# Shifting one ring of weight buffers by 64 bytes in the on-chip memory

## The chip, the cores and the metric

The kernel runs on one core of a Trainium2 chip. A core has a matrix engine (TensorE, PE in the profile; its weight loads are listed apart as PEld), a vector engine (VectorE, DVE), an activation engine (ScalarE, ACT), a general engine (GpSimd, POOL) and a queue engine that issues transfers (SyncE, SP). They work from an on-chip memory of 128 partitions (SBUF); TensorE writes its results to a second one (PSUM). The metric is the device time of one execution in microseconds, as the median of several runs; lower is better.

## The reference

A retention layer (attention without softmax, with a decay mask) feeds two feed-forward layers one after the other:

```python
def _attn_ref(q, k, v):                       # (4, 8, 576, 64) each
    scores = scale * np.matmul(q, k.transpose(0, 1, 3, 2))
    Dmat = np.where(rel >= 0, gamma[:, None, None] ** rel[None, :, :], 0.0)
    return np.matmul(scores * Dmat[None, :, :, :], v)

def _moe_ref(x, w_in, w_out):                 # x (2304, 512), w_in (512, 2048), w_out (2048, 512)
    h = x @ w_in
    return np.maximum(0.01 * h, h) @ w_out

def _moe2_ref(x, w_in, w_out):
    h = x @ w_in
    return (h - np.tanh(h)) @ w_out
```

The weights come as 64-bit floats; everything else is 32-bit.

## The kernel before

**Precision.** Each product of the two feed-forward layers is made of three matmuls in the one-pass form of 32-bit floats: a number is split into a high part (rounded to that form) and the rest, and high by high, high by rest and rest by high are added up in PSUM. So a split weight piece is a tile `wp` of 128 partitions x 2 x 512 floats: `wp[:, 0, :]` is the high part, `wp[:, 1, :]` the rest. Input activations stand split too, in `xh` and `xl`; the hidden layer's in `g`.

**Stages.** `retention()` handles 16 pairs of heads. For each it loads `qk` and `kv`, scales them on GpSimd, makes scores, masks them, and writes the result into `xh` and `xl`. From the fifth pair on it also runs pieces of the first feed-forward layer in blocks of 256 tokens (`unit_h`, L520, and `unit_o`, L545), as soon as the tokens are there. `layers()` then walks a list of steps: a step is one block of 512 or 256 tokens by one of the 16 slices of 128 hidden units; four slices make a group. `h_mm` (L195) makes 12 matmuls with a slice of `wp` as the stationary operand and `xh` or `xl` as the moving one. In the first layer `o_mm` (L267) has `wp` stationary and `g` moving; in the second the roles are exchanged, `g` stationary and the whole 512 columns of a `wp` half moving.

**The ring of split weights.** `split_piece` (L172 to L179) fills a tile of the pool `wring`: ScalarE writes the high part (L175), GpSimd reads the raw piece and the high part and writes the rest (L176). The pool has four buffers of each of two tags (`w0` for the incoming weights, `w1` for the outgoing ones), 4,096 bytes per partition each, 32,768 bytes in all. 64 pieces pass through it. Raw pieces (64-bit) are loaded into `st` (two buffers, L110) and turned into 32-bit floats in `cw` by VectorE; some are parked in memory (`kept`, L164) and fetched again (L169).

**Where buffers stand.** Pools are laid one behind the other in the order in which they are opened: `keep` (`qb`, `xh`, `xl`, `acc`, for the whole program), `wring`, `stage` (`st`), and then the pools of the stage that runs. All sizes in `keep` and behind it are multiples of 128 bytes per partition (`LINE` is 32 floats; small tables are rounded up to it), so every tile begins on a multiple of 128 bytes. The ring begins at byte 127,232 of each partition, which is 994 x 128. Slices of a tile that TensorE reads begin at further multiples of 256 bytes.

**Order.** Every engine works off its instructions in the order in which the code issues them; no scheduler changes it.

Of the kernel before, what the change touches and what calls it, by code (L numbers as in the profile page):

```python
# [10 lines left out]
F32 = mybir.dt.float32  # L11
# [7 lines left out]
P = 128  # L19
LINE = 32  # L20
# [14 lines left out]
def retention_moe_moe(  # L35
# [28 lines left out]
    keep = ctx.enter_context(tc.tile_pool(name="keep", bufs=1))  # L64
    wring = ctx.enter_context(tc.tile_pool(name="wring", bufs=GF))
    stage = ctx.enter_context(tc.tile_pool(name="stage", bufs=2))
# [2 lines left out]
    xh = keep.tile([P, KK, NT], F32R, name="xh")  # L69
    xl = keep.tile([P, KK, NT], F32R, name="xl")  # L70
    acc = keep.tile([P, KK * NT], F32, name="acc")
    acc_t = acc.rearrange("p (d t) -> p d t", d=KK)
    acc_n = acc.rearrange("p (t e) -> p t e", e=DM)

# [692 lines left out]
```

## Time and profile before

| | before |
|---|---|
| median of 3 runs | 894.48 us (893.25 to 894.73) |
| profiled execution, whole | 892.59 us |
| its span, first to last instruction | 890.8 us |
| TensorE matmul busy | 865.0 us, 97% |
| TensorE weight load busy | 741.6 us, 83% |
| VectorE / ScalarE / GpSimd busy | 60% / 42% / 47% |
| mean granted TensorE clock | 0.996 of full speed |

The span is the time between the first and the last instruction; 1.8 us of the execution lie outside it. The busy share of TensorE says little by itself, since matmuls overlap their neighbours' ends; the step from one matmul's start to the next is read from the chain of waits, which gives a stretch of equal matmuls as one piece with its length and count.

### The profile page before, as it was taken

What the parts mean: (1) busy time and instruction counts of PE and PEld (TensorE: products, weight loads), DVE (VectorE), ACT (ScalarE), POOL (GpSimd) and SP (SyncE); (2) the same over time, 40 slices, a digit from 0 to 9 for tenths busy, and PEclk for the clock granted to TensorE, in tenths of its full rate; (3) what the DMA queues carried; (4) which work ended last, traced back from release to release, by engine and by line L of the source; (5) the groups of instructions that cost most, each with busy time, mean ns of one, the idle gap of its engine ahead of it and who ended that gap; (6) DMA issues with size and microseconds to landing.
All of it is one profiled execution on the core that took longest, in us unless ns stands there. A gap on an engine that the chain in (4) does not pass through costs nothing.

```text
span 890.8 us, 13456 instructions
## 1 busy us (share of the span) xinstructions
PE 865.0 (97%) x5152; PEld 741.6 (83%) x5152; DVE 534.9 (60%) x880; ACT 374.5 (42%) x751; POOL 423.0 (47%) x340
## 2 busy tenths in 40 slices
PE   6669999999999999999999999999999999999998
PEld 6659999988888889888888888888888888888886
DVE  6964334698888788875652555444545655555454
ACT  2333222243122212233324656675466555565553
POOL 4544432264223622363224644585457744585443
PEclk9989999999999999999999999999999999999999
DMA  8633332223465345631121200020001000001111
GB/s 301 239 130 124 107 120 90 71 96 118 130 179 152 109 134 148 178 107 48 47 83 36 60 1 1 3 78 15 1 1 47 13 1 1 1 1 48 48 48 71
DMA packets 28575, 70.97 MB, mean 80 GB/s; under 512 B 3296, under 2 KB 3680, under 8 KB 28512
## 3 DMA queue, kind: packets, MB, share of 16 engines
q1 hardware_dynamic: 27936, 69.74, 24.3%
q8 instruction: 40, 0.66, 0.3%
q10 hardware_dynamic: 576, 0.38, 0.1%
q14 instruction: 23, 0.19, 0.1%
HBM read 59.10 MB, written 11.01 MB: 79 GB/s over the span
## 4 chain that ended last, share of the span: by engine, by line
PE 92%; DVE 3%; ACT 1%; DMA 1%; POOL 1%; issue 1%; SPq 0%; POOLq 0%; ACTq 0%
PE h L195 40%; PE a L267 40%; PE a L545 4%; PE x_b L520 3%; PE sc L406 1%; PE o L467 1%; PE o L479 1%; DVE cw L149 1%; DVE pt L421 1%; DMA kv<-in_vn 1%; POOL wp L176 1%; PE x_c L439 1%; DMA qk<-in_qT 0%; PE x_a L412 0%; DVE st L449 0%
## 5 line engine op out<-in xcount | busy, mean ns | idle before, releaser
L195 PE MATMUL h<-xh,wp 128*128 128x512 f32 (+1 forms) x1184 | 355.2, 366 | 0.0
L195 PEld LDWEIGHTS h<-xh,wp 128*128 128x128 f32 x1184 | 216.1, 189 | 36.8
L195 PE MATMUL h<-xl,wp 128*128 128x512 f32 (+1 forms) x592 | 216.9, 366 | 0.0
L267 PE MATMUL a<-wp,g 128*128 128x512 f32 x864 | 209.4, 390 | 0.2 <-POOL g L241 0.2
L267 PEld LDWEIGHTS a<-wp,g 128*128 128x128 f32 x864 | 161.1, 188 | 33.8 <-POOL g L241 1.0
L267 PE MATMUL a<-g,wp 128*128 128x512 f32 (+1 forms) x816 | 175.6, 364 | 0.0
L241 POOL TENSOR_TENSOR g<-v,g 128x512 fp32r<-128x512 f32 (+1 forms) x80 | 95.0, 1187 | 144.7 <-ACT g L240 144.6
L267 PEld LDWEIGHTS a<-g,wp 128*128 128x128 f32 x816 | 141.4, 189 | 24.6
L241 POOL TENSOR_TENSOR g<-a,g 128x512 fp32r<-128x512 f32 (+1 forms) x68 | 88.3, 1298 | 154.7 <-ACT g L209 141.3
L208 ACT ACTIVATE a<-h 128x512 f32<-128x512 f32 (+1 forms) x68 | 37.3, 549 | 227.0 <-PE h L195 226.0
L176 POOL TENSOR_TENSOR wp<-cw,wp 128x512 fp32r<-128x512 f32 x64 | 91.2, 1434 | 76.5 <-ACT wp L175 76.3
L195 PEld LDWEIGHTS h<-xl,wp 128*128 128x128 f32 x592 | 111.6, 189 | 18.6
L149 DVE SCALAR_TENSOR_TENSOR cw<-st,cw 128x512 uint32<-128x512 uint32 x128 | 116.9, 913 | 3.8
L234 DVE TENSOR_TENSOR h<-h,t 128x512 f32<-128x512 f32 (+1 forms) x80 | 51.5, 644 | 107.2 <-ACT t L218 107.2
L293 DVE TENSOR_TENSOR acc<-a,acc 128x512 f32<-128x512 f32 (+1 forms) x114 | 73.8, 663 | 65.2 <-PE a L267 65.2
L240 ACT ACTIVATE g<-v 128x512 fp32r<-128x512 f32 (+1 forms) x80 | 47.1, 589 | 145.4 <-DVE v L238 144.2
L219 POOL TENSOR_TENSOR v<-t,u 128x512 f32<-128x512 f32 (+1 forms) x80 | 94.8, 1185 | 14.0 <-ACT t L218 13.6
L235 DVE SCALAR_TENSOR_TENSOR v<-q,v 128x512 f32<-128x512 f32 (+1 forms) x80 | 55.6, 695 | 55.2 <-POOL v L219 54.2
L238 DVE COPY_PREDICATED v<-mk,h 128x512 f32<-128x512 uint32 (+1 forms) x80 | 55.0, 687 | 8.2
L220 ACT ACTIVATE q<-u,qb 128x512 f32<-128x512 f32 (+1 forms) x80 | 54.5, 681 | 0.0
L223 ACT ACTIVATE mk<-u,qb 128x512 f32<-128x512 f32 (+1 forms) x80 | 54.2, 678 | 0.0
L132 DVE TENSOR_SCALAR cw<-st 128x512 uint32<-128x512 uint32 x56 | 39.0, 696 | 22.0 <-DMA st<-in_w2i 8.5
(60 smaller groups left out, 781.1 us busy)
## 6 DMA issues: line engine op xcount, KB each, us to landing
st<-in_w1i SPq DMA_DIRECT2D x16, 512.0 KB, 3.7
st<-in_w1o SPq DMA_DIRECT2D x16, 512.0 KB, 3.4
st<-in_w2i SPq DMA_DIRECT2D x16, 512.0 KB, 3.9
st<-in_w2o SPq DMA_DIRECT2D x16, 512.0 KB, 3.9
kept<-cw SPq DMA_DIRECT2D x24, 256.0 KB, 4.2
cw<-kept SPq DMA_DIRECT2D x24, 256.0 KB, 2.6
kv<-in_vn SPq DMA_DIRECT2D x16, 320.0 KB, 4.9
qk<-in_qT SPq DMA_DIRECT2D x16, 288.0 KB, 3.7
```

The lines of the kernel that those rows point to most:

```text
L149: nc.vector.scalar_tensor_tensor(out=t["w"], in0=t[src], scalar=scalar, in1=t["w"], op0=op, op1=ALU.bitwise_or)
L176: nc.gpsimd.tensor_tensor(out=wp[:, 1, :], in0=wf, in1=wp[:, 0, :].bitcast(F32), op=ALU.subtract)
L195: nc.tensor.matmul(out=ps[:, :n], lhsT=w[:, wi, cs], rhs=x[:, kk, t0:t0 + n], start=kk == 0 and i == 0, stop=kk == KK - 1 and i == 2,)
L219: nc.gpsimd.tensor_tensor(out=v[:, :n], in0=t_[:, :n], in1=u[:, :n], op=ALU.mult)
L220: nc.scalar.activation(out=q[:, :n], in_=u[:, :n], func=AF.Square, scale=math.sqrt(RHO_C), bias=qb[:, 0:1])
L223: nc.scalar.activation(out=mk[:, :n], in_=u[:, :n], func=AF.Relu, bias=qb[:, 1:2])
L234: nc.vector.tensor_tensor(out=h, in0=h, in1=t_, op=ALU.subtract)
L235: nc.vector.scalar_tensor_tensor(out=v, in0=q, scalar=RHO_A, in1=v, op0=ALU.add, op1=ALU.mult)
L238: nc.vector.copy_predicated(out=v, mask=mk.bitcast(U32), data=h)
L241: nc.gpsimd.tensor_tensor(out=gt[:, 1, :n], in0=v, in1=gt[:, 0, :n].bitcast(F32), op=ALU.subtract)
L267: nc.tensor.matmul(out=o, lhsT=l, rhs=r, start=f == 0 and i == 0 and d % pack == 0, stop=f == GF - 1 and i == 2 and (d + 1) % pack == 0, s ...
L293: nc.vector.tensor_tensor(out=dst, in0=a, in1=dst, op=ALU.add)
```

## The change

Two small tiles that nothing writes or reads are added, 64 bytes per partition each:

```diff
@@ -69,6 +69,8 @@
     xh = keep.tile([P, KK, NT], F32R, name="xh")
     xl = keep.tile([P, KK, NT], F32R, name="xl")
     acc = keep.tile([P, KK * NT], F32, name="acc")
+    keep.tile([P, LINE // 2], F32, name="shift")
+    stage.tile([P, LINE // 2], F32, name="unshift", bufs=1)
     acc_t = acc.rearrange("p (d t) -> p d t", d=KK)
     acc_n = acc.rearrange("p (t e) -> p t e", e=DM)
```

The first stands at the end of `keep`, so the ring behind it begins at byte 127,296, 64 bytes behind a multiple of 128. The second stands at the beginning of `stage`, so `st` and all that follows moves by 128 bytes in all and begins on multiples of 128 as before. `qb`, `xh`, `xl` and `acc` stay where they were. One thing else shifts with it: what begins on a multiple of 256 bytes behind the ring (`st`, `g` and `cw` of the layers) begins on an odd multiple of 128 afterwards, and the other way round (`qk` and `kv` of the retention stage). No instruction is added, removed or moved on any engine; line numbers behind the two lines grow by 2.

## Rows read from the trace of the kernel before

**Rows 1.** The page's busy times, and the clock in 40 slices.

```profile
PE 865.0 (97%) x5152; PEld 741.6 (83%) x5152; DVE 534.9 (60%) x880; ACT 374.5 (42%) x751; POOL 423.0 (47%) x340
PEclk9989999999999999999999999999999999999999
```

**Rows 2.** Busy time by stretch: us, engines with counts, granted clock, DMA share, GB/s.

```profile
0.00:163.00 163.00, 141.31 (x1694) 132.02 (x1695) 84.14 (x212) 48.09 (x125) 67.84 (x56) 0.98 0.45 152
163.00:891.00 728.00, 723.68 (x3460) 609.60 (x3459) 450.79 (x668) 326.42 (x626) 355.13 (x284) 1.00 0.20 63
...
40.00:90.00 50.00, 41.14 (x464) 38.19 (x463) 29.28 (x63) 16.40 (x41) 24.23 (x20) 0.93 0.40 131
```

**Rows 3.** TensorE's waits: who for whom, us in total, times, longest.

```profile
PE a L545 <- ACT wp L175: 4.9, 1, 4.9
...
PE a L267 <- POOL g L241: 0.2, 1, 0.2
```

**Rows 4.** The chain that ended last: start us, us, line, count of matmuls.

```profile
76.00 2.87 PE x_b L520 x24
78.86 2.85 PE a L545 x24
185.93 2.72 PE h L195 x12
188.65 2.72 PE a L267 x12
...
605.01 2.72 PE a L267 x12
```

**Rows 5.** Matmuls by line and shape: count, busy us, mean ns.

```profile
L195 PE MATMUL h<-xh,wp 128*128 128x512 f32 x928 | 304.6, 389 | 0.0
...
L267 PE MATMUL a<-wp,g 128*128 128x512 f32 x864 | 209.4, 390 | 0.2 <-POOL g L241 0.2
L195 PE MATMUL h<-xl,wp 128*128 128x512 f32 x464 | 180.6, 389 | 0.0
L267 PE MATMUL a<-g,wp 128*128 128x512 f32 x624 | 150.1, 389 | 0.0
L195 PE MATMUL h<-xh,wp 128*128 128x256 f32 x256 | 50.6, 282 | 0.0
L545 PE MATMUL a<-g,wp 128*128 128x256 f32 x288 | 38.4, 289 | 5.5 <-ACT wp L175 4.9 <-POOL wp L176 0.6
L520 PE MATMUL x_b<-xh,wp 128*128 128x256 f32 x192 | 37.7, 289 | 2.1 <-ACT g L528 1.1 <-POOL wp L176 0.9
L195 PE MATMUL h<-xl,wp 128*128 128x256 f32 x128 | 36.2, 283 | 0.0
L520 PE MATMUL x_b<-xl,wp 128*128 128x256 f32 x96 | 27.2, 283 | 0.0
L267 PE MATMUL a<-g,wp 128*128 128x256 f32 x192 | 25.6, 283 | 0.0
```

**Rows 6.** The same view of the first 163 us: the two writers of the ring.

```profile
L176 POOL TENSOR_TENSOR wp<-cw,wp 128x512 fp32r<-128x512 f32 x8 | 10.3, 1288 | 17.9 <-ACT wp L175 17.9
L175 ACT ACTIVATE wp<-cw 128x512 fp32r<-128x512 f32 x8 | 5.0, 631 | 2.8 <-DVE cw L149 2.7
```

**Rows 7.** GpSimd's scaling of kv: count, shortest, median and longest ns.

```profile
L383 POOL TENSOR_TENSOR kv<-kv,vt_sb x16: 1257/1260/1704, 7.7 to 138.0; 128x640 f32<-128x640 f32 x16
```

**Rows 8.** Transfers: count, KB each, median us to landing.

```profile
st<-in_w1i SPq DMA_DIRECT2D x16, 512.0 KB, 3.7
```

**Rows 9.** The chain's first two transfers: start us, us.

```profile
2.11 5.46 DMA kv<-in_vn
...
14.78 4.42 DMA qk<-in_qT
```

**Rows 10.** A weight load and its matmul, in order of time: start us, us.

```profile
300.75 0.19 PEld L195 LDWEIGHTS h<-xl,wp 128*128 128x128 f32 x1
...
300.98 0.39 PE L195 MATMUL h<-xl,wp 128*128 128x512 f32 x1
```

## The prediction

> **What bounds the kernel now.** I read the page's busy line first: TensorE 97%, the next engine 60%, and a granted clock at full speed in all slices but one or two near the start [rows 1]. Then busy time by stretch, which parts the span in two. In the 728 us from 163 us on, TensorE is busy 723.7 us, at a granted clock of 1.00, which is 2.4 GHz; the 163 us before are the mixed stage, with 141 us of TensorE work at 0.98 [rows 2]. Then TensorE's waits: the longest in which the ring has a part is one of 4.9 us in the first stage, for ScalarE's L175; the layers have a single one of 0.2 us [rows 3]. So from 163 us on nothing but TensorE's own pace sets the end, and the chain of waits gives that pace: 12 matmuls of 512 columns in 2.72 us, 226.7 ns each, for L195 and for L267, in the first layer (`wp` stationary, at 188 us) and in the second (`wp` moving, at 605 us); 24 matmuls of 256 columns in 2.87 or 2.85 us, 119.6 or 118.8 ns each [rows 4].
>
> At 2.4 GHz 512 columns take 213.3 ns and 256 take 106.7 ns. So a matmul costs its columns and 12 to 13.3 ns more, whatever its width; 13.3 ns are 32 columns. The pace is the same for a stationary operand from `wp` and from `g`, and for a moving one from `xh`, `g` and `wp`.
>
> **What the ring touches.** From the counts by shape [rows 5]: `wp` is stationary in 928 + 464 + 256 + 128 = 1,776 matmuls of L195, 624 + 192 = 816 of L267, 288 of L545 and 192 + 96 = 288 of L520, together 3,168; it is moving in 864 of L267. That is all 4,032 matmuls of the two layers: 2,880 of 512 columns at 226.7 ns and 1,152 of 256 at 119.6 ns, 652.9 + 137.8 = 790.7 us, 89% of the span. The price of a slower or faster read of `wp` is thus multiplied by thousands: one column more per matmul (0.417 ns) is 1.7 us, just under the 0.2% (1.8 us) that a measurement of this kernel can tell from no change.
>
> **The change, part by part.**
>
> No instruction is added or moved, so there is no term for work. What is left are four places where a start 64 bytes behind a multiple of 128 could cost or give something. No row of before has a matmul operand that starts there, so each is bounded from its neighbours.
>
> 1. Stationary reads, 3,168 times 512 bytes per partition: four whole pieces of 128 bytes before, three whole and two halves after. Lower end: the whole surcharge of 13.3 ns goes, -42 us. Upper end, if every piece is straddled and the surcharge doubles: +42 us. Nearest rows: `g` of L545 stands, by the sizes of what is laid ahead of it, on odd multiples of 128 bytes, the `g` of the layers and `xh` on multiples of 256, and the first is read at 118.8 ns, the second kind at 119.6 ns (L520's `xh`) [rows 4]. Another phase by 128 bytes moves nothing by even one column, and the pace holds to a column over all the slices of `xh`, `xl`, `g` and `wp`. I take 0.
>
> 2. Moving reads, 864 times 2,048 bytes: 16 pieces before, 17 touched after. If each touched piece cost its own time, a sixteenth of 213.3 ns, 13.3 ns x 864 = +11.5 us. At the other end, if half of the surcharge went, -5.8 us. The exchange of roles between the layers, at an unchanged 2.72 us, says that the pace hangs on the count of columns and not on which buffer is streamed. I take 0.
>
> 3. The writers. ScalarE writes 64 high parts and GpSimd reads and writes 64 pieces. From 163 us on both engines have slack (326 and 355 of 728 us busy [rows 2]), and nobody waits. In the first stage there are eight of each, 5.0 and 10.3 us [rows 6], and TensorE does wait for them, 4.9 us once for L175 [rows 3]. If a seventeenth piece cost a sixteenth more and all of it were on the path: 15.3 / 16 = +1.0 us; the same less is the lower end. There is a nearby row for GpSimd: the second operand of L383 is a table whose slices start 0, 40, 80 and 120 bytes behind a multiple of 128 for the four head pairs, and of its 16 calls the shortest takes 1,257 ns and the median 1,260 [rows 7]. I take 0.
>
> 4. Transfers. Nothing is transferred into the ring, but `st` moves from multiples of 256 bytes to odd multiples of 128, and `qk` and `kv` the other way. In the layers no transfer is waited for. In the first stage the chain holds 5.46 us of `kv` and 4.42 us of `qk` [rows 9]; eight loads of `st` with a median of 3.7 us to landing [rows 8] run two pieces ahead. The landing times of the two kinds differ by size and company and do not show the start address by itself. If a ninth piece of 256 bytes cost `kv` and `qk` a ninth until now, they give back 9.9 / 9 = 1.1 us; if `st` now pays a sixteenth on all eight, 29.6 / 16 = +1.9 us. I take 0, with -1.1 and +1.9 as ends.
>
> The first stage has one more lever: from 40 to 90 us the granted clock is 0.93, which is 3.5 us' worth at full speed, and TensorE has 8.9 us without work there [rows 2]. Were those waits a little longer or shorter, the loss of clock could double or go: 3.5 us either way, from tenths of a microsecond in parts 3 and 4. I give that a twentieth, shared by both sides.
>
> [...]
>
> Sum: the profiled execution took 892.6 us (890.8 us of span and 1.8 around it); it changes by 0, with small ends of about -2 and +3 from parts 3 and 4. That execution lies 1.9 us below the median of the runs, 894.5 us, so the median forecast is 894.5 us.
>
> **The rivals.**
>
> *Slower: a stationary operand that straddles lines.* The 32 columns of surcharge are a quarter of the 128 columns that a load brings, and 512 bytes in four pieces of 128 would be one way to come by a quarter. If a load is fetched in such pieces and the surcharge is the exposed part of it, five pieces instead of four cost 3.3 ns more, on 3,168 matmuls 10.6 us: 905 us. It decides from one column per matmul on. For it speaks that the surcharge is independent of the width; against it, that a weight load starts 0.23 us ahead of its matmul, beside the matmul before it, and that the step of 119 ns between narrow matmuls is shorter than the 0.19 us that a load shows [rows 4, 10], so loads overlap and a small delay could be swallowed. With the moving reads at their upper end as well it would be 917 us.
>
> [...]
>
> *Faster: the two read streams were in each other's way.* If the surcharge were a clash of the weight load with the moving operand, because both begin on the same multiple of 128, a half-step apart would relieve it. Half of it on the 3,168 would be -21 us, 873 us; all of it 852 us. For it: the surcharge is exactly as long as a quarter of the load. Against it: a clash should vary with the streams' phases, which run through all multiples of 128 and 256 here, and it never varies; and in the second layer `g` against `wp` meets the same 226.7 ns.
>
> *The change does nothing to the ring*: excluded by the layout, since the ring begins at 127,296.
>
> **How the numbers follow.** No change 0.56: the pace is independent of buffer and phase wherever rows can show it. Slower 0.27, most of it the straddling load, some the moving reads and the first stage. Faster 0.17, most of it the clash, some the first stage. The likeliest alone spans 892 to 897 us. For eight in ten the range goes up to 906, which takes in the price of one piece more per load, and down to 887, which takes in a relief of a sixth of the surcharge and all of the first stage's ends; about a tenth is left out on each side.
>
> **What would show it.** Right: in the chain after, 12 matmuls of L197 and of L269 still take 2.72 us in both layers, and the stretch from 163 us on is 728 us long. The slower rival shows as 2.76 us per 12 of L197 and of the first layer's L269, but 2.72 for the second layer's L269 if only stationary reads pay; the moving term shows in that last row alone. The faster one shows as 2.64 us or less. Parts 3 and 4 show in the means of L177 and L178 and in the start of the first full stretch. A pace off by more than a column in any of these rows proves the forecast wrong.

## The result and the profile after

The change makes the kernel slower: 904.88 us (904.14 to 906.04) against 894.16 us, ratio 1.0122 (1.0104 to 1.014). The profiled execution took 904.17 us with a span of 902.4 us, 11.6 us more than before.

The page's busy line looks much as it did, and so do the waits for the ring and in the layers [rows 1, 3]. The largest shift among TensorE's waits is in the first stage, for GpSimd's two scalings of `qk` and `kv`: 7.2 and 4.8 us instead of 5.8 and 3.9, and that stage ended sooner all the same. No wait has come that would carry 10 us:

```profile
PE 875.5 (97%) x5152; PEld 737.0 (82%) x5152; DVE 529.7 (59%) x880; ACT 376.1 (42%) x751; POOL 421.9 (47%) x340
```

```profile
PE a L547 <- ACT wp L177: 5.0, 1, 5.0
...
PE a L269 <- POOL g L243: 0.2, 1, 0.2
```

The pace has changed. The chain of waits of the kernel after (start us, us, line, count of matmuls), in the first stage, the first layer with a block of 256 columns, and the second layer:

```profile
86.22 2.75 PE x_b L522 x24
88.97 2.72 PE a L547 x24
...
161.95 4.12 PE h L197 x35
...
228.71 2.79 PE h L197 x12
231.50 2.75 PE a L269 x12
234.25 1.41 PE h L197 x12
...
604.41 2.80 PE a L269 x12
```

The same view of the kernel before, for the pieces that were not shown there:

```profile
163.47 2.63 PE h L195 x22
...
234.89 1.43 PE h L195 x12
236.33 2.75 PE a L267 x12
```

A stretch of twelve equal matmuls is called a dozen below. Against [rows 4]: twelve matmuls of 512 columns went from 2.72 us to 2.79 (L197), 2.75 (L269 of the first layer, `wp` stationary) and 2.80 (L269 of the second, `wp` moving); they are called wide below, those of 256 columns narrow. Those of 256 columns became *faster*: 24 in 2.75 and 2.72 us instead of 2.87 and 2.85, twelve in 1.41 instead of 1.43. The 2.4 GHz of the prediction stands in no row; the two paces of before give a column 0.418 ns, (226.7 - 119.6) / 256 [rows 4], if what comes on top is the same at both widths, so 2.4 columns per ns is an estimate from them. By it a dozen has, in columns beyond the matmul's own (us per dozen x 200, less 512 or 256), which I call the surcharge: 46, 38 and 48 where 32 stood, 16 to 19 in the first stage where 29 to 31 stood. The levels hang on that estimate, the differences hardly. The layers now last from 161.95 to 902.4, 740.4 us instead of 727.3: 13.1 us more. The first stage ends 1.5 us earlier. That is the 11.6.

The ring's writers and the transfers did not move. The writers in the first stage (by shape), and a transfer:

```profile
L178 POOL TENSOR_TENSOR wp<-cw,wp 128x512 fp32r<-128x512 f32 x8 | 10.3, 1286 | 20.7 <-ACT wp L177 20.7
L177 ACT ACTIVATE wp<-cw 128x512 fp32r<-128x512 f32 x8 | 5.0, 630 | 2.8 <-DVE cw L151 2.7
```

```profile
st<-in_w1i SPq DMA_DIRECT2D x16, 512.0 KB, 3.6
```

The means are 1,286 and 630 ns against 1,288 and 631 [rows 6], and 3.6 us to landing against 3.7 [rows 8].

### The profile page after: what moved, and what is told of

Read it like the earlier page. It is cut to its first block, busy times and chain, and to the rows that moved or that the text cites. A ratio compares the mean times of both kernels' runs of the same rounds, so it can differ in the third digit from the quotient of the medians.

```text
span 902.4 us, 13456 instructions
## 1 busy us (share of the span) xinstructions
PE 875.5 (97%) x5152; PEld 737.0 (82%) x5152; DVE 529.7 (59%) x880; ACT 376.1 (42%) x751; POOL 421.9 (47%) x340
## 4 chain that ended last, share of the span: by engine, by line
PE 93%; DVE 4%; ACT 1%; POOL 1%; issue 1%; DMA 1%; SPq 0%; ACTq 0%; POOLq 0%
PE h L197 41%; PE a L269 40%; PE a L547 3%; PE x_b L522 3%; PE o L481 1%; PE o L469 1%; PE sc L408 1%; DVE cw L151 1%; DVE pt L423 1%; DMA kv<-in_vn 1%; POOL wp L178 1%; PE x_c L441 1%; PE x_a L414 0%; DVE st L451 0%; DVE xl L491 0%
## 5 line engine op out<-in xcount | busy, mean ns | idle before, releaser
L197 PE MATMUL h<-xh,wp 128*128 128x512 f32 (+1 forms) x1184 | 359.1, 369 | 0.0
L197 PEld LDWEIGHTS h<-xh,wp 128*128 128x128 f32 x1184 | 215.1, 188 | 42.0
L197 PE MATMUL h<-xl,wp 128*128 128x512 f32 (+1 forms) x592 | 218.7, 369 | 0.0
L269 PE MATMUL a<-wp,g 128*128 128x512 f32 x864 | 214.4, 395 | 0.2 <-POOL g L243 0.2
L269 PEld LDWEIGHTS a<-wp,g 128*128 128x128 f32 x864 | 160.5, 187 | 38.8 <-POOL g L243 1.0
L269 PE MATMUL a<-g,wp 128*128 128x512 f32 (+1 forms) x816 | 176.8, 365 | 0.0
L269 PEld LDWEIGHTS a<-g,wp 128*128 128x128 f32 x816 | 141.0, 188 | 26.5
L197 PEld LDWEIGHTS h<-xl,wp 128*128 128x128 f32 x592 | 111.1, 188 | 21.9
L151 DVE SCALAR_TENSOR_TENSOR cw<-st,cw 128x512 uint32<-128x512 uint32 x128 | 114.3, 893 | 3.8
L237 DVE SCALAR_TENSOR_TENSOR v<-q,v 128x512 f32<-128x512 f32 (+1 forms) x80 | 51.4, 643 | 51.2 <-POOL v L221 50.2
L219 ACT ACTIVATE u<-h 128x512 f32<-128x512 f32 (+1 forms) x80 | 43.8, 547 | 31.1 <-PE h L197 25.9
```

The source lines that it names most:

```text
L151: nc.vector.scalar_tensor_tensor(out=t["w"], in0=t[src], scalar=scalar, in1=t["w"], op0=op, op1=ALU.bitwise_or)
L197: nc.tensor.matmul(out=ps[:, :n], lhsT=w[:, wi, cs], rhs=x[:, kk, t0:t0 + n], start=kk == 0 and i == 0, stop=kk == KK - 1 and i == 2,)
L237: nc.vector.scalar_tensor_tensor(out=v, in0=q, scalar=RHO_A, in1=v, op0=ALU.add, op1=ALU.mult)
L269: nc.tensor.matmul(out=o, lhsT=l, rhs=r, start=f == 0 and i == 0 and d % pack == 0, stop=f == GF - 1 and i == 2 and (d + 1) % pack == 0, s ...
```

## The experiments

Below, the **distance** of a matmul is the start of its stationary operand minus that of its moving one, in bytes within a partition. Before, it was a multiple of 256 for every matmul of the layers. The change made it +64 for L197 and for the second layer's L269, but -64 for the first layer's L269, because `g` moved by 128 as well. In the first stage it was 0 for L520 and an odd multiple of 128 for L545; the change made it +64 for both.

**Everything by 64 bytes.**

```diff
+    keep.tile([P, 16], F32, name="first")
     qb = keep.tile([P, LINE], F32, name="qb")
```

> Everything from the first buffer on begins 64 bytes behind a multiple of 128, the ring too; the distances between buffers are those of the kernel before. Theory A (own start: a read that begins 64 bytes behind a multiple of 128 costs, whatever is read beside it): stationary and moving operands all begin there, so at least the 904.9 us of the change, 233 ns per 512-column matmul in both layers. Theory R (distance: what counts is how far the stationary operand's start lies from the moving one's, modulo 128 or 256 bytes): the distances are as before, so 894 us, 226.7 ns per 512 columns and 119 to 120 ns per 256.

Measured: 893.93 us, ratio to before 1.0007 (0.9997 to 1.0016). Its chain in the first and second layer:

```profile
299.80 2.72 PE a L268 x12
302.52 2.72 PE h L196 x12
...
601.14 2.72 PE a L268 x12
```

Every stationary and moving operand of the layers now begins 64 bytes behind a multiple of 128, and nothing is lost. Theory A falls.

**Only what stands behind the ring.**

```diff
+    stage.tile([P, 32], F32, name="unshift", bufs=1)
     acc_t = acc.rearrange("p (d t) -> p d t", d=KK)
```

> Only the side effect of the change: the ring stays where it was, and what stands behind it moves by 128 bytes. Theory A: nothing begins off a multiple of 128, so 894 us and 226.7 ns everywhere. Theory R with a period of 128 bytes: the same. Theory R with a period of 256: L195 keeps 226.7 ns, but L267, where g is now 128 bytes off the ring, leaves it in both layers; the change's 229 ns in the first layer's L269 would then be the move of g, and the time 892 to 900 us.

Measured: 904.02 us, ratio 1.0122 (1.0102 to 1.0143): as slow as the change, without moving the ring at all.

```profile
88.77 2.88 PE a L546 x24
...
300.15 2.79 PE a L268 x12
302.94 2.73 PE h L196 x12
...
600.11 2.80 PE a L268 x12
602.91 2.76 PE h L196 x12
```

In the layers L268, at distance -128 and +128, pays 46 to 48 columns. So 128 is not a period. L196, with its distance of 0, is at 34 and 40: 32 is its pace at that distance where L267 stands at 0 too [rows 4]; here its dozens stand between L268's disturbed ones. Row one is the first stage's second product, which the run brought from 128 to 0: 2.88 us where 2.85 stood [rows 4], so that narrow matmuls take 32 columns at 0 and 29 at 128. The time lies above the 892 to 900 that I expected, since I had counted `g` for the 229 ns of the change alone.

**The ring by 64, the rest by 512.**

```diff
+    keep.tile([P, 16], F32, name="shift")
+    stage.tile([P, 112], F32, name="unshift", bufs=1)
```

> The ring begins 64 bytes later, what stands behind it 512, so that g, qk, kv and st keep their place within any 512 bytes. Theory A: as the change, 905 us; 233 ns for L195, 229 for the first layer's L267 and 233 for the second's. Theory R: the distance stationary minus moving is +64 for L195 and the first layer's L267, and -64 (192) for the second layer's; the change had +64, -64 and +64. So the two layers' L267 should exchange their paces, 233 ns in the first and 229 in the second; time about 905, since 624 matmuls gain 4 ns against 864 that lose 4.

Measured: 905.61 us, ratio 1.014 (1.0123 to 1.0157).

```profile
87.80 2.83 PE x_b L522 x24
...
97.48 2.74 PE x_b L522 x24
...
301.53 2.80 PE a L269 x12
304.33 2.80 PE h L197 x12
...
599.78 2.80 PE h L197 x12
602.59 2.76 PE a L269 x12
```

The two layers' L269 exchanged their paces as expected: 2.80 at +64, 2.76 at -64, whichever operand comes from the ring. In the first stage, the narrow L522 at +64 takes 27 and 18 columns in turn, beside L547 at -64, where the change with both at +64 had 19: for narrow matmuls the own distance alone does not set the pace.

**The ring by 32, the rest by 512** (8 and 120 floats in the same two lines).

> As the run with 64, but the ring begins 32 bytes later. Theory A: 32 bytes off is as much a straddle as 64, so about 905 us; or, if pieces of 64 bytes count, the same. Theory R: the surcharge of a matmul follows the distance in columns (8 columns for 32 bytes, 3.3 ns), up or down: 223.3 or 230 ns per 512 columns in L195 and the first layer's L267, the other way round in the second layer's; time between 884 and 904 us.

Measured: 910.7 us, ratio 1.0199 (1.0179 to 1.0218). A miss: +32 and -32 both take 48 columns, not 40 or 24, so the surcharge does not follow the distance column by column.

```profile
299.90 2.80 PE h L197 x12
302.70 2.80 PE a L269 x12
...
599.84 2.80 PE a L269 x12
```

**The ring by 256, the rest by 512** (64 and 64 floats).

> The ring begins 256 bytes later, the rest behind it 512: every distance between a stationary and a moving operand of the layers becomes 256 bytes. The run that moved only the rest by 128 has shown that 128 is not a period. If the period of the distance is 256 bytes, this is the kernel before: 893 us, 226.7 ns per 512 columns everywhere. If it is 512 or more, the pace leaves 226.7 ns in L195 and L267 as at the other distances seen, 550 to 560 columns, 229 to 233 ns: 900 to 907 us. Theory A (own start) expects 893 us, but has failed already in the run that moved everything.

Measured: 892.85 us, ratio 0.9997 (0.9985 to 1.0009).

```profile
300.63 2.72 PE h L197 x12
303.35 2.72 PE a L269 x12
...
604.76 2.72 PE a L269 x12
```

At 256 the pace of 0 is back, 2.72 us a dozen, and at 128 it was 2.79 and 2.80: of the distances tried, 256 bytes is the period.

**Other distances**, three in each of four runs. The ring stays where it was modulo 256 bytes; `xh`, `xl` and `g` are shifted inside larger tiles, here as in the first of the four, where `at` is 104:

```diff
-    xh = keep.tile([P, KK, NT], F32R, name="xh")
+    xh = keep.tile([P, KK * NT + 128], F32R, name="xh")
+    xh = xh[:, 124:124 + KK * NT].rearrange("p (k t) -> p k t", k=KK)
...
+        room = pools["g"].tile([P, 2 * W + 128], F32R, tag="g", name="g")
+        return room[:, at:at + 2 * W].rearrange("p (i n) -> p i n", i=2)
```

> The ring and all else stays; the moving operands are moved within larger tiles, so that the distance stationary minus moving is +16 bytes in L195, +96 in the first layer's L267 and -96 in the second's. Under the theory of distances each class has a pace of its own, whatever its neighbours do. If only a distance of 0 is good, all three lie at 229 to 234 ns per 512 columns and the time at 900 to 910 us. If a distance lets the load through at 16 columns instead of 32, as the 256-column matmuls at +64 show, that class falls to 220 ns: 9 us less for L195, 4 to 6 us for one of L267.

> As the run before it, with distances of -16 bytes in L195, +192 in the first layer's L267 and -192 in the second's. If a distance of 16 bytes, one row of four columns, is near enough to 0, L195 stays at 226.7 ns; if the effect is sharp, 229 to 234. For the others 229 to 234 ns, or 226.7 or less if the distances between 128 and 256 hold a good one. Time 893 to 910 us.

> As the two before it, with distances of +160 bytes in L195, 256 in the first layer's L267 and -160 in the second's. The 256 must agree with the run that moves the ring by 256: if the period is 256 the first layer's L267 keeps 226.7 ns while the others leave it; else all three leave it, 229 to 234 ns. Time 895 to 910 us.

> As the runs with distances before, with -48 bytes in L195, -80 in the first layer's L267 and +80 in the second's. The distances seen so far give, in columns beyond 512: 32 at 0, 48 at 16 to 96, 46 to 50 at 128 and 160, 37 to 40 at -64, 47 at -32, 44 at -16. If -64 lies in a dip, -48 and -80 lie near 38 to 44 columns; if it is a point by itself, near 47. For a gain on the kernel before one of them would have to lie under 32. Time 900 to 910 us.

Measured, ratios to before: 911.78 us, 1.0203 (1.0181 to 1.0225); 903.85 us, 1.0116 (1.0092 to 1.0139); 909.56 us, 1.0179 (1.0158 to 1.0199); 908.01 us, 1.017 (1.0151 to 1.0188). One dozen of L195's line and one of each layer's L267's, from the chain of each of the four in turn:

```profile
302.14 2.80 PE a L274 x12
304.95 2.81 PE h L202 x12
...
604.99 2.79 PE a L274 x12
```

```profile
302.04 2.78 PE h L202 x12
304.82 2.75 PE a L274 x12
...
604.84 2.80 PE a L274 x12
```

```profile
300.70 2.76 PE a L274 x12
303.46 2.81 PE h L202 x12
...
608.49 2.79 PE a L274 x12
```

```profile
302.29 2.80 PE h L202 x12
305.08 2.77 PE a L274 x12
...
606.86 2.79 PE a L274 x12
```

Columns beyond 512, from these dozens and those above (one column is 0.005 us of a dozen, so each is good to one or two):

| distance modulo 256 | -96 | -80 | -64 | -48 | -32 | -16 | 0 | 16 | 32 | 64 | 80 | 96 | 128 |
|---|---|---|---|---|---|---|---|---|---|---|---|---|---|
| columns | 46 to 50 | 42 | 38 to 40 | 48 | 48 | 44 | 32 | 50 | 48 | 46 to 48 | 46 | 46 to 48 | 46 to 48 |

At none of the 13 distances does a wide matmul go below 32. The effect is sharp: the dozens at 16 bytes off stand at 50 and 44 columns, those at 128 at 46 to 48. The 256 of the third run came out at 2.76 us and not 2.72, beside dozens of L202 at 2.81; by the run with the ring moved by 256, where every wide dozen shown takes 2.72, I put that down to the neighbours. Such a dozen at 0 reaches 42 columns in the last run below, so the 42 at -80 and the 44 at -16, measured beside other disturbed dozens, are not shown to be these distances' own. The 40 at -64 are, and the 48 at +64: in the last run those dozens stand beside dozens at 0, as those at 128 do in the run that moved only the rest.

**Only the low halves.**

```diff
-        wp = wring.tile([P, 2, 512], F32R, tag=f"w{key[1]}", name="wp")
+        room = wring.tile([P, 1024 + 64], F32R, tag=f"w{key[1]}", name="wp")
+        wp = (room[:, :512], room[:, 528:1040])
```

> Only the low half of each split weight tile begins 64 bytes later; high halves and all moving operands but the second layer's low halves stay. In L195 three matmuls repeat: high by xh, high by xl, low by xh. Theory R1 (the distance that counts is that of the next load from the stream that runs beside it): the step from the second matmul to the third is lengthened, since the low half is loaded beside the second stream. Theory R2 (the distance of a matmul's own two operands): the step from the third to the next is lengthened. One in three at distance 64 costs at most 16 columns: 2,880 / 3 x 6.7 ns = 6.4 us, so 893 to 900 us, unless the pattern unsettles the steps between as well.

Measured: 904.74 us, ratio 1.0125 (1.011 to 1.0141): a third of the matmuls displaced costs as much as all. TensorE in order of time, the end of a dozen; the last row but one is a low half:

```profile
305.14 0.62 PE L196 MATMUL h<-xh,wp 128*128 128x512 f32 x2
305.61 0.39 PE L196 MATMUL h<-xl,wp 128*128 128x512 f32 x1
305.83 0.40 PE L196 MATMUL h<-xh,wp 128*128 128x512 f32 x1
306.07 1.31 PE L268 MATMUL a<-g,wp 128*128 128x512 f32 x5
```

The low half's own step is the long one here, 0.24 us where 0.227 is undisturbed, and the one ahead of it, in which the low half is loaded, is 0.22. A dozen of L196 takes 2.77 us in the chain:

```profile
303.46 2.77 PE h L196 x12
```

That is 13 ns more per triple, and rows good to 10 ns cannot place them. The starts in the trace can, as means over the first layer's whole dozens of L196: the three steps of a triple take 229.2, 229.6 and 234.6 ns. The step in which the low half is loaded, R1's mark, is no longer than the one before it; the low half's own step, R2's mark, has 8 of the 13 ns. So a matmul's own two operands carry most of it, and the other two steps 2.5 and 2.9 ns, whose cause is open. The time lies above the 900 us that I allowed, since the rest of the triple is unsettled too.

**A version for speed**, with distance 0 for 512 columns and +64 for most of 256:

```diff
+    WIDE = NT - NT % 512
+    SHIFT = 48
...
+            room[:, :main].rearrange("p (k t) -> p k t", k=KK),
+            room[:, at:at + KK * (NT - WIDE)].rearrange("p (k t) -> p k t", k=KK),
...
+            if n < W:
+                gt = gt[:, :, SHIFT:]
```

> A version for speed: matmuls of 512 columns keep the distance 0, those of 256 columns get +64 bytes where the layout lets them. The last 256 tokens of xh and xl stand 192 bytes behind a multiple of 256 from the ring's phase, g of the first layer's 256-token blocks likewise, and g of the first stage's units moves by 64 bytes. The eight writes that cross the border of the last 256 tokens are done in two parts. Theory R: 576 matmuls of 256 columns in the layers fall from 31 columns of surcharge to 18 to 20 (3 us), 288 of L545 by some 10 (1 us): 889 us, 0.4% faster. Theory A has no reason for a gain: 893 us.

Measured: 890.43 us, ratio to before 0.9968 (0.9956 to 0.998), the fastest of all.

```profile
89.55 2.74 PE a L567 x24
...
232.01 2.72 PE a L283 x12
234.73 1.41 PE h L209 x12
```

L545's units, at 128 before, fell from 2.85 to 2.74 us (12 of them, 1.3 us), the layers' narrow dozens from 1.43 to 1.41, less than the 18 to 20 columns expected; and the wide dozens beside them from 2.75 to 2.72. 2.8 us of the expected 4.

**The change with `xh` and `xl` moved along** (16 floats inside larger tiles, as above).

> The change, with xh and xl moved by 64 bytes as well, so that L197 has its distance of 0 back and nothing else differs from the change (904.9 us). Theory of distances: L197 falls from 46 to 47 columns beyond 512 to 32 where it is undisturbed; in the run that moved only the rest by 128, with both L268 at 46 columns, L196 kept 36 and 39 on the mean, since the first matmuls of each dozen start out of step. By these, 624 x 10 + 768 x 8 columns = 5.2 us less, and 384 narrow matmuls at 30 columns instead of 23 to 26, 0.9 us more: about 900.5 us, 899 to 902. Theory A (own start): xh and xl now begin 64 bytes behind a multiple of 128, so slower than the change, over 905 us.

Measured: 903.54 us, ratio to before 1.0097 (1.0076 to 1.0118).

```profile
300.39 2.76 PE a L271 x12
303.15 2.77 PE h L199 x12
...
600.28 2.80 PE a L271 x12
603.08 2.75 PE h L199 x12
```

The direction is that of the theory of distances, the size is not: L199, at 0, falls to 42 and 38 columns, not 32; L271 around it stays at 40 (distance -64) and 48 (+64), and I put the rest down to that company, as in the run that moved only the rest. The interval overlaps the change's, so this run alone does not show a gain.

## Why the prediction was right and wrong

The time lies inside the range of 887 to 906 us, but the likeliest case, no change at 0.56, is not what came; slower had 0.27. That the range holds it is luck: its upper end came from the price of the straddling load, which is not what happened. By the signs that the prediction gave itself, a pace off by more than a column, it is wrong in mechanism.

*The bound and the price of a column: right.* TensorE's pace alone sets the end from 163 us on, where its one wait is 0.2 us before and after, and 13.1 us of change stand in that stretch.

*"Another phase by 128 bytes moves nothing by even one column": the step that failed* (part 1, "I take 0"). It compared L545's `g` with L520's `xh`, both read by narrow matmuls, at 118.8 and 119.6 ns. Those 0.8 ns are already two columns, not less than one, and the one at 128 is the faster. Wide matmuls lose 14 to 16 columns at a distance of 128, as the run that moved only the rest shows. The other support, that the pace holds over all slices of `xh`, `xl`, `g` and `wp`, held no information: those starts differ by multiples of 256 bytes, so the distance was 0 in every one of the 2,880 wide matmuls.

*Part 2, moving reads at 0: failed too*, for the same reason. The second layer's L269 pays 0.08 us a dozen, 72 dozens, 5.8 us; its ground, that "the pace hangs on the count of columns and not on which buffer is streamed", is true of the buffer but not of where it begins.

*Parts 3 and 4, writers and transfers: right*, at 0. The time of `st` to landing, 3.6 us against 3.7, shows no price of its new start. No run shows the pieces of 256 bytes from which the ends of part 4 were worked out, -1.1 and +1.9 us: the other loads of `st` kept their 3.4, 3.9 and 3.9 us, and those of `kv` and `qk`, which should have gained, took 4.9, 4.5, 3.8 and 4.3 us where 4.9, 4.4, 3.7 and 4.6 stood. That the loss of clock hangs on TensorE's waits, the lever of 3.5 us, was an estimate that no run shows either: from 40 to 90 us the granted clock was 0.93 again, with 7.7 us without work where 8.9 stood. The first stage did change, by -1.5 us. Its narrow matmuls saved 0.12 and 0.13 us on most of the 12 units each of L522 and L547, which is more than that in all. But the run that moved everything, at the paces of before, entered the layers at 165.08 us, 1.6 later than before, so the cause of a shift of this size is not shown. The longest wait for the ring stayed, 5.0 us against 4.9.

*The slower rival hit 905 us by accident.* It priced 3.3 ns on 3,168 stationary reads, 10.6 us. In its place: +0.07 us on 116 dozens of L197 (8.1 us), +0.03 on 52 of the first layer's L269 (1.6), +0.08 on 72 of the second's (5.8), and 0.01 to 0.06 us less on each of the 48 narrow dozens of the layers; by the dozens some 14 us in the layers, by the stretch 13.1, since a few dozens beside narrow blocks stood at 2.75 before. Its own marks, 2.76 for both uses as stationary and 2.72 for the use as moving, are not met. And with every read straddling, in the run that moved everything, nothing is lost (ratio 1.0007). So no run shows a price of 3.3 ns for a load that straddles one piece of 128 bytes more, the term that this rival was worked out from.

*The faster rival had the right quantity and the wrong sign.* The two reads do depend on each other, by their distance. But 0 is the best of the 13 distances for 512 columns, and the relief it hoped for was seen with 256 columns only (24 in 2.75 and 2.72 us instead of 2.87 and 2.85). What I held against it, that the phases "run through all multiples of 128 and 256 here" and the pace never varies, was wrong in its premise: for the wide matmuls the distance was always a multiple of 256.

Why the distance counts, and why a wide and a narrow matmul want different ones, no run shows. That it does, with a period of 256 bytes, rests on three runs: all buffers moved together cost nothing (ratio 1.0007), the ring moved by 256 cost nothing (0.9997), and what stands behind the ring moved by 128 cost what the change did (1.0122).

## What to carry to other kernels

Where every matmul loads its own weights, check how far stationary and moving operands lie apart modulo 256 bytes, not whether each begins on a round address; for this form of matmul the pace between starts (a dozen in the chain) tells it at once (here 2.72 us at 0, 2.75 to 2.81 at the others). A pad ahead of one buffer moves everything behind it: the control is to move only that, and here it cost as much as the change (904.02 us against 904.88). And a number that never varies in a profile says nothing about a quantity that never varied with it.

## What the runs showed of the hardware

- A matmul of 128 x 512 of the kernel's 32-bit floats (`F32R`) with its own weight load steps at 226.7 ns (2.72 us a dozen, 512 + 32 columns) at a granted clock of 1.00 and a distance of 0 modulo 256 bytes, and at 229 to 234 ns (2.75 to 2.81 us a dozen, 512 + 38 to 50 columns) at the 12 others tried, though at -80 and -16 part of it may be the neighbours'. Moving both operands by 64 bytes changes nothing (2.72 us a dozen, ratio 1.0007).
- With 256 columns, in the first stage, 24 matmuls take 2.87 and 2.88 us at 0 (31 to 32 columns beyond 256) and 2.85 at 128 (29); with both products at +64 they take 2.75 and 2.72 us, 16 to 19 columns (the change). With the first product at +64 and the second at -64 (the ring by 64, the rest by 512), the second takes 2.83 us (27) and the first 2.83 and 2.74 (27 and 18) in turn.
- The pace of a dozen goes with its neighbours' too: dozens at distance 0 beside disturbed ones take 2.73 to 2.77 us instead of 2.72 (the runs that moved only the rest, that tried +160 and 256, and the last).
